# Two phases' projection work from a written list, and GpSimd multiplies and adds in a two-branch attention kernel

## The chip, the core and the metric

The kernel runs on one core of one Trainium2 chip. The metric is the device time of one execution in microseconds (us). TensorE is called PE below, VectorE DVE, ScalarE ACT, GpSimd POOL, and SyncE, whose queue issues nearly all DMAs, SP.

## What is computed

Two attention branches read two inputs of 2048 rows by 640 columns (bf16), each with 32 heads of 20 columns. Their outputs stand side by side.

```python
# branch A, for each of N = 4 segments of 512 rows
p     = softmax(q @ k.T * 20**-0.5 + causal mask within the segment)
a_dot = p @ v
pq    = phi(q)                              # t + 1 where t > 0, else exp(t)
a_mem = (pq @ M) / (pq @ z + 1e-6)
o     = g * a_mem + (1 - g) * a_dot         # g = sigmoid(beta), one per head
M, z  = M + phi(k).T @ v, z + phi(k).sum()  # M and z start at zero
# branch B
p = softmax of q @ k.T * 20**-0.5 over the last 256 rows up to the own one
o = p @ v
# each: o.reshape(2048, 640) @ wo
```

## The kernel before

**Phases, packs, slots.** Both branches are cut into 4 chunks of 512 rows. `body` (line 720) goes through eight phases in the order B0, A0, B1, A1, B2, A2, B3, A3. A phase's score work is cut into packs of up to 512 columns for four heads at once: 20 packs in B0 and in each A phase, 24 in B1 to B3. One turn of the loop over packs (line 739) is a slot, 172 in all; `self.slot` counts them. B0 has slots 0-19, A0 20-39, B1 40-63, A1 64-83, B2 84-107, A2 108-127, B3 128-151, A3 152-171.

**A slot.** It runs what was due in `self.after` (line 744), then the scores of its pack (`scores`, line 483), what stands in `self.behind`, one `weigh` if a unit (four heads of a chunk) has been complete for two slots, what stands in `last_of`, and then other work. `scores` issues 4 to 8 matmuls into two of three PSUM tiles `Sc`, two exponentials of 128x1024 on ACT (line 497) and the masks on POOL (lines 511, 517). `weigh` (line 527) multiplies the exponentials with v, copies the result from PSUM to SBUF on DVE (line 562; 577 in chunk 0), and SP transposes it by DMA. Four to six slots later `normalise` (line 591) divides: a reciprocal on DVE (595), a multiply (601) and, in A after chunk 0, an add of the memory's part `omem` (611). The multiply is on POOL in A1, A2 and A3 (`self.remembering`), on DVE elsewhere; the add is on DVE always, two to five groups of columns at once, at set groups.

**The other work.** It is a list per phase, `dense`, of pieces with a cost in us and sometimes a slot by which they are due, made by `plan` (line 385):

- `proj_padded` and `proj_rest` (lines 239, 263): B0's k and q.
- `proj` (line 287): one of five parts of k or q of a later chunk, five matmuls of 512 columns (A's are written Ak0 to Ak4 and Aq0 to Aq4 here, B1's Bk0 to Bq4). DVE copies it from PSUM (line 296), SP stores it to DRAM (297), and two slots after certain parts `spread` (line 306) loads groups of heads back in four DMAs, in the layout that the scores read. `cut` (line 298) says after which part which groups are loaded.
- `phi` (line 319): for A, one more exponential on ACT and two DVE operations per part, and for k a transposing DMA into `pkt`.
- `vproj` (line 349): one v tile of 128x320, DVE copies it.
- `load_x` (line 105): the next chunk's x, transposed by one DMA. Its tile has a single buffer per branch.

Two more kinds are kept apart: the memory's reads (`read`, line 447; eight in each of A1 to A3) and updates (`upd`, line 427; five per chunk of A but the last), and the output projection `out_half` (line 624). In each slot `body` takes as many pieces of the three kinds as `pick` (line 788) finds to fit best to a running sum of the costs; pieces that are due come first. So the order within a phase follows from costs and due slots.

**Queues and buffers.** Every engine and SP's queue run in program order. All these matmuls but the scores write to one kind of PSUM tile, `D`, with two buffers (line 235): the third writer waits for the copy of the first.

Of the kernel before, what the change touches and what calls it, by code (L numbers as in the profile page):

```python
# [8 lines left out]
ALU = mybir.AluOpType  # L9
# [8 lines left out]
G = 8  # L18
GW = 4 * DH
KT = 5  # L20
NC = 4
CH = 512
CT = CH // P
# [59 lines left out]
class Kern:  # L83
# [203 lines left out]
    def proj(self, br, c, which, m, st):  # L287
        nc = self.nc
        if m == 0:
            st[which] = self.dram.tile([KT * P, CH], BF16, name="%sd%s" % (which, br), bufs=2)  # L290
        ps = self.dtile([P, CH], F32)
        for kt in range(KT):
            nc.tensor.matmul(ps[:], lhsT=self.w[br + which][:, kt, m * P:(m + 1) * P],  # L293
                             rhs=self.xT[br][:, kt, :], start=(kt == 0), stop=(kt == KT - 1))
        t = self.wk.tile([P, CH], BF16, name="qk", bufs=4)
        nc.vector.tensor_copy(out=t[:], in_=ps[:])  # L296
        nc.sync.dma_start(out=st[which][m * P:(m + 1) * P, :], in_=t[:])
        cut = {1: (0, 3), 3: (3, 6), 4: (6, 8)} if (br, c) in (("A", 0), ("B", 1)) else {4: (0, 8)}
        if (br, c) == ("A", 1):
            cut = {2: (0, 4), 4: (4, 8)}  # L300
        if m in cut:
            self.at(self.slot + 2, lambda: self.spread(br, c, which, st, *cut[m]))
        if br == "A":
            self.phi(c, which, m, t, st)
# [80 lines left out]
    def plan(self):  # L385

        def kq(g, due):
            return [(1.25, lambda which=which: self.proj_padded(which, g), due) for which in "kq"]

        st = {}  # L390
        sr = {}

        def rest(what, due):
            return [(1.19, lambda: self.proj_rest(what, sr), due)]

        A = {(w, m): [self.a_kq("A", 0, w, m, st, {4: 9}.get(m))]
             for w in "kq" for m in range(KT)}
        stB = {}
        B = self.atoms_qk("B", 1, stB, True)
        upd = {c: [] for c in range(NC)}  # L400
        upd[0] = self.a_upd(0, st)
        v1 = self.a_v("B", 1, 0, 4)
        mix = [x for pair in zip(v1, upd[0]) for x in pair] + upd[0][4:]
        lists = [kq(0, 0) + kq(1, 2) + self.a_v("B", 0, 0, 4) + kq(2, 5) + rest("k0", 6)
                 + rest("q0", 6) + kq(3, 7) + rest("k1", 8) + rest("q1", 8) + rest("kq", 9)
                 + A["k", 0] + A["k", 1] + A["q", 0] + self.a_v("B", 0, 1, 14) + A["q", 1] + A["k", 2]
                 + A["q", 2] + A["k", 3] + A["q", 3],
                 self.a_v("A", 0, 0, 4) + self.a_x("B", 1) + A["k", 4] + A["q", 4]
                 + self.a_v("A", 0, 1, 14) + self.a_x("A", 1) + B,
                 [(x[0], x[1], 4) for x in mix]]  # L410
        for n in range(2, 7):
            br, c = "AB"[n % 2], (n + 1) // 2
            st = {}
            more = self.atoms_qk(br, c, st) + self.atoms_v(br, c)
            if br == "A":
                upd[c] = self.a_upd(c, st)
            if n == 2:
                more = (self.atoms_qk(br, c, st, True)[:6] + self.a_v("B", 1, 1, 13) + self.a_x("B", 2)
                        + self.atoms_qk(br, c, st, True)[6:] + self.atoms_v(br, c))
                lists[2] = lists[2] + more  # L420
            else:
                lists.append(more)
        return lists + [[]], upd
# [3 lines left out]
    def upd(self, c, m, st):  # L427
        nc = self.nc
        h0 = P * m // DH
        n = (P * (m + 1) - 1) // DH - h0 + 1  # L430
        W = DH + 1
        ps = self.dtile([P, 8, W], F32)
        for tt in range(CT):
            nc.tensor.matmul(ps[:, 0:n, :], lhsT=st["kt"][:, m, tt, :],
                             rhs=self.v["A"][0][:, tt, h0:h0 + n, 0:W],
                             start=(tt == 0), stop=(tt == CT - 1))
        if m == 0:
            self.mz[c] = self.wk.tile([P, KT, 8, W], BF16, name="mz", bufs=2)
        acc = self.macc[:, m, 0:n, :]
        bmb = self.bm[:, m, 0:n].unsqueeze(2).to_broadcast([P, n, W])  # L440
        if c == 0:
            nc.vector.tensor_copy(out=acc, in_=ps[:, 0:n, :])
        else:
            nc.vector.tensor_tensor(out=acc, in0=ps[:, 0:n, :], in1=acc, op=ALU.add)
        nc.vector.tensor_tensor(out=self.mz[c][:, m, 0:n, :], in0=acc, in1=bmb, op=ALU.mult)

    def read(self, c, tt, hf):
        nc = self.nc
        if tt == 0 and hf == 0:
            self.omem = self.io.tile([P, CT, D], BF16, name="omem", bufs=1)  # L450
        W = DH + 1
        ps = self.dtile([P, 16 * W], F32)
        cols = []
        for m in range(KT):
            h0 = P * m // DH
            h1 = (P * (m + 1) - 1) // DH
            prev = (P * m - 1) // DH if m else -1
            a, b = max(h0, 16 * hf), min(h1, 16 * hf + 15)
            if a > b:
                continue  # L460
            if a == prev and any(x[2] == prev for x in cols):
                cols.append((m, a, a, h0))
                a += 1
            if a <= b:
                cols.append((m, a, b, h0))
        for n, (m, a, b, h0) in enumerate(cols):
            nc.tensor.matmul(ps[:, (a - 16 * hf) * W:(b + 1 - 16 * hf) * W],
                             lhsT=self.phiq[:, m, tt * P:(tt + 1) * P],
                             rhs=self.mz[c - 1][:, m, a - h0:b + 1 - h0, :],
                             start=(n == 0), stop=(n == len(cols) - 1))  # L470
        pv = ps[:].rearrange("p (h e) -> p h e", e=W)
        hs = slice(16 * hf, 16 * hf + 16)
        rr = self.wk.tile([P, 16], F32, name="rm", bufs=2)
        nc.vector.scalar_tensor_tensor(out=rr[:], in0=pv[:, :, DH], scalar=EPS,  # L474
                                       in1=self.ge[:, hs], op0=ALU.add, op1=ALU.mult)
        nc.vector.reciprocal(out=rr[:], in_=rr[:])
        nc.vector.tensor_tensor(  # L477
            out=self.omem[:, tt, 320 * hf:320 * hf + 320].rearrange("p (h e) -> p h e", e=DH),
            in0=pv[:, :, 0:DH], in1=rr[:].unsqueeze(2).to_broadcast([P, 16, DH]), op=ALU.mult)
# [111 lines left out]
    def normalise(self, u, tp, a=0, n=CT):  # L591
        nc = self.nc
        pv = tp.rearrange("p b (j c) -> p b j c", j=4)
        rr = self.wk.tile([P, CT, 4], F32, name="rr", bufs=2)
        nc.vector.reciprocal(out=rr[:, 0:n, :], in_=pv[:, :, :, DH])
        if u.g == 0:
            self.o_tok[u.br, u.c] = self.io.tile([P, CT, D], BF16, name="ot" + u.br, bufs=2)
        o = self.o_tok[u.br, u.c][:, a:a + n, :]
        cols = slice(GW * u.g, GW * (u.g + 1))
        eng = nc.gpsimd if self.remembering else nc.vector  # L600
        eng.tensor_tensor(out=o[:, :, cols].rearrange("p b (j e) -> p b j e", j=4),
                          in0=pv[:, :, :, 0:DH],
                          in1=rr[:, 0:n, :].unsqueeze(3).to_broadcast([P, n, 4, DH]),
                          op=ALU.mult)
        if u.br == "A" and u.c > 0:
            c0 = {3: 0, 5: 4, 7: 6}.get(u.g, u.g + 1)
            if u.c == NC - 1:
                c0 = 0 if u.g == G - 4 else u.g if u.g > G - 4 else u.g + 1
            cols = slice(GW * c0, GW * (u.g + 1))
            if cols.stop > cols.start:  # L610
                nc.vector.tensor_tensor(out=o[:, :, cols], in0=o[:, :, cols],
                                        in1=self.omem[:, a:a + n, cols], op=ALU.add)
        if u.g == G - 1 and n == CT:
            self.tiles += [(u.br, u.c, tt) for tt in range(CT)]


# [103 lines left out]
    def body(self):  # L720
        phases = [Phase(br, c) for c in range(NC) for br in "BA"]
        lists, upd = self.plan()
        self.turned, self.half = [], []
        self.closing, self.open_masks = False, []
        for n, ph in enumerate(phases):
# [13 lines left out]
            for i, pk in enumerate(ph.packs):  # L739
# [20 lines left out]
                    f()  # L760
                if outs or i >= np_ - 3:
                    self.prefetch()
                part = sum(weights[:i + 1]) / sum(weights)
                can = 2 * sum(1 for t in self.turned if t[0] + 2 <= self.slot) + len(self.half)
                room, ahead, due = total * part - done, 0.0, 0.0
# [6 lines left out]
                for kind in self.pick(part, room, dense[at[0]:at[0] + 3],  # L772
# [5 lines left out]
                    else:  # L778
                        a = (dense, mem)[kind][at[kind]]
# [113 lines left out]
```

## Time and profile before

| what | value |
|---|---|
| three timed runs | 376.49, 377.37, 377.96 us; median 377.37 |
| profiled execution | 376.41 us, of which 374.7 are the span from the first to the last instruction |
| granted TensorE clock, mean | 0.995 |
| busy in slots 0-19 (10.33 to 54.27 us) | PE 41.85, ACT 36.35, DVE 28.20, POOL 29.84 of 43.94 |
| slots 20-39 (to 91.94) | PE 35.59, ACT 37.65, DVE 24.15, POOL 20.64 of 37.67 |
| slots 40-63 (to 142.92) | PE 45.95, ACT 49.22, DVE 42.22, POOL 41.05 of 50.98 |
| slots 64-83 (to 184.12) | PE 36.63, ACT 37.83, DVE 29.36, POOL 25.63 of 41.20 |
| slots 108-127 (233.22 to 274.11) | PE 36.37, ACT 37.77, DVE 29.07, POOL 25.59 of 40.89 |
| slots 152-170 (322.57 to 359.93) | PE 33.04, ACT 35.27, DVE 24.91, POOL 25.67 of 37.36 |

The stretches are cut where ACT's first exponential of a slot begins. Busy is the time in which an engine ran an instruction; a PE that is busy is not always at its peak, since matmuls overlap. A line of the timeline gives the start, the length, the engine, the line of the code, the operation with the tile it writes and the tiles it reads, how many were merged, and in brackets how long the engine had been idle before it and what ended that wait. A line of the waits gives who waited for whom, the total, how often, and the longest.

### The profile page before, as it was taken

The numbers are of one execution on the slowest core, as the hardware profiler recorded it, in microseconds if no ns is written. First come the engines' busy times: TensorE is split into PE (matmuls) and PEld (weight loads), VectorE is DVE, ScalarE is ACT, GpSimd is POOL, SyncE is SP. The second block draws the span as 40 slices with busy tenths as digits, with TensorE's granted clock in tenths as the row PEclk, the third lists the DMA queues.
The fourth block names the chain that finished last, engine by engine and source line by source line (L and its number), as shares of the span: only waits on it lengthen the run. The fifth ranks groups of instructions, "written<-read, shape, count | busy, mean of one in ns | idle before, by whom it ended". The sixth has DMA issues, their size and how long they took to land.

```text
span 374.7 us, 10400 instructions
## 1 busy us (share of the span) xinstructions
PE 337.9 (90%) x3930; PEld 159.5 (43%) x3930; DVE 261.7 (70%) x562; ACT 338.1 (90%) x386; POOL 262.2 (70%) x414
## 2 busy tenths in 40 slices
PE   8999999999898988898989999889899999989876
PEld 4443433433434344444434345334444444544444
DVE  2456767566888788866689877777567785776554
ACT  2778989999899998999899999999899999999943
POOL 9667675555786977566688889556678888766650
PEclk9999999999999999999999999999999999999989
DMA  8964457576434958566575976728644769465512
GB/s 250 311 231 118 115 162 167 120 197 155 129 98 136 175 129 161 158 111 128 83 174 131 198 125 112 155 58 154 114 86 119 140 156 114 97 133 118 131 41 73
DMA packets 112242, 52.08 MB, mean 139 GB/s; under 512 B 81856, under 2 KB 112192, under 8 KB 112192
## 3 DMA queue, kind: packets, MB, share of 16 engines
q1 hardware_dynamic: 112048, 51.33, 61.6%
q8 instruction: 31, 0.51, 0.6%
q14 instruction: 19, 0.16, 0.2%
q10 hardware_dynamic: 144, 0.08, 0.1%
HBM read 17.05 MB, written 15.07 MB: 86 GB/s over the span
## 4 chain that ended last, share of the span: by engine, by line
PE 45%; ACT 30%; DVE 11%; issue 6%; DMA 5%; POOL 2%; POOLq 0%; ACTq 0%; DVEq 0%
ACT pt L497 27%; PE D L293 14%; PE Sc L491 8%; PE D L353 5%; PE D L546 5%; PE D L630 4%; DMA ocT<-oc 3%; ACT pe L337 3%; DVE qk L296 2%; PE D L255 2%; DMA oT<-otB 2%; DVE oc L562 2%; PE Sc L674 1%; PE D L275 1%; DVE omem L477 1%
## 5 line engine op out<-in xcount | busy, mean ns | idle before, releaser
L497 ACT ACTIVATE pt<-Sc 128x1024 bf16<-128x1024 f32 (+1 forms) x344 | 321.4, 1072 | 19.9 <-PE Sc L491 18.7
L511 POOL TENSOR_SCALAR_AFFINE_SELECT pt<-pt 128x512 bf16<-128x512 bf16 x254 | 165.7, 664 | 94.3 <-ACT pt L497 93.9
L517 POOL TENSOR_SCALAR_AFFINE_SELECT pt<-pt 128x512 bf16<-128x512 bf16 x112 | 75.9, 691 | 3.4 <-ACT pt L497 3.1
L296 DVE CAST qk<-D 128x512 bf16<-128x512 f32 x70 | 48.2, 688 | 34.0 <-PE D L293 33.7
L491 PE MATMUL Sc<-qpB,kpB 20*128 20x256 bf16 (+2 forms) x704 | 47.8, 276 | 7.3 <-ACT pt L497 5.5
L562 DVE CAST oc<-D 128x512 bf16<-128x512 f32 x46 | 31.7, 690 | 16.5 <-PE D L546 16.1
L491 PE MATMUL Sc<-qpA,kpA 20*128 20x384 bf16 (+3 forms) x512 | 38.1, 301 | 2.7 <-ACT pt L497 2.3
L491 PEld LDWEIGHTS <-kpB 20*128 20x128 bf16 x704 | 15.1, 92 | 44.3 <-issue 42.9
L630 PEld LDWEIGHTS <-oT 128*128 128x128 bf16 x280 | 24.7, 98 | 20.0 <-issue 7.8
L633 DVE CAST ot<-D 128x320 bf16<-128x320 f32 x56 | 27.1, 486 | 7.5 <-PE D L630 6.5
L353 PE MATMUL D<-Bv,xTB 128*128 128x320 bf16 x160 | 25.5, 300 | 5.0 <-DVE oc L562 3.0
L630 PE MATMUL D<-Bo,oT 128*128 128x320 bf16 x160 | 26.5, 301 | 2.5 <-DMA oT<-otB 1.9
L546 PE MATMUL D<-pt,vB 128*32 128x384 bf16 (+2 forms) x720 | 26.3, 275 | 1.0 <-DVE qk L296 0.9
L293 PE MATMUL D<-xTA,Ak 128*128 128x512 bf16 x100 | 25.0, 381 | 1.8 <-DVE oc L562 1.8
L353 PE MATMUL D<-Av,xTA 128*128 128x320 bf16 x160 | 26.3, 301 | 0.3 <-DVE vA L361 0.2
L293 PE MATMUL D<-xTA,Aq 128*128 128x512 bf16 x100 | 25.0, 381 | 0.6 <-DVE phiq L577 0.3
L546 PE MATMUL D<-pt,vA 128*32 128x256 bf16 (+3 forms) x576 | 23.9, 291 | 1.5 <-DVE pkt L668 1.5
L491 PEld LDWEIGHTS <-kpA 20*128 20x128 bf16 x512 | 11.3, 92 | 30.6 <-issue 29.3
L630 PE MATMUL D<-Ao,oT 128*128 128x320 bf16 x120 | 20.2, 300 | 1.5 <-DVE rm L474 0.9
L337 ACT ACTIVATE pe<-qk 128x512 bf16<-128x512 bf16 x30 | 21.0, 704 | 0.0
L293 PE MATMUL D<-xTB,Bk 128*128 128x512 bf16 x75 | 18.7, 380 | 2.3 <-DVE omem L477 1.9
L353 PEld LDWEIGHTS <-xTB 128*128 128x128 bf16 x160 | 14.4, 97 | 14.0 <-issue 9.3
(103 smaller groups left out, 368.7 us busy)
## 6 DMA issues: line engine op xcount, KB each, us to landing
out_dram<-ot SPq DMA_DIRECT2D x31, 160.0 KB
kdA<-qk SPq DMA_DIRECT2D x20, 128.0 KB
qdA<-qk SPq DMA_DIRECT2D x20, 128.0 KB
kdB<-qk SPq DMA_DIRECT2D x17, 128.0 KB
qdB<-qk SPq DMA_DIRECT2D x17, 128.0 KB
kpB<-kdB SPq DMA_DIRECT2D x8, 160.0 KB
qpB<-qdB SPq DMA_DIRECT2D x8, 160.0 KB
kpA<-kdA SPq DMA_DIRECT2D x8, 160.0 KB
```

The source lines that it names most:

```text
L293: nc.tensor.matmul(ps[:], lhsT=self.w[br + which][:, kt, m * P:(m + 1) * P], rhs=self.xT[br][:, kt, :], start=(kt == 0), stop=(kt == KT - 1))
L296: nc.vector.tensor_copy(out=t[:], in_=ps[:])
L337: nc.scalar.activation(out=e[:], in_=t[:], func=ACT.Exp)
L353: nc.tensor.matmul(ps[:, 0:320], lhsT=self.xT[br][:, kt, tt * P:(tt + 1) * P], rhs=self.w[br + "v"][:, kt, hf * 320:(hf + 1) * 320], start ...
L491: nc.tensor.matmul(ps[j // 2][:, j % 2, off * P:(off + nq) * P], lhsT=kp[rows, u.g, k0:k0 + P], rhs=self.qp[u.br][rows, u.g, q0 * P:(q0 + ...
L497: nc.scalar.activation(out=pt[:, 2 * hp:2 * hp + 2, 0:pk.used], in_=ps[hp][:, :, 0:pk.used], func=ACT.Exp, scale=SCALE)
L511: nc.gpsimd.affine_select(out=blk, in_=blk, pattern=[[0, 4], [1, P]], compare_op=ALU.is_ge, fill=0.0, base=0, channel_multiplier=-1)
L517: nc.gpsimd.affine_select(out=blk, in_=blk, pattern=[[0, 4], [-1, P]], compare_op=ALU.is_ge, fill=0.0, base=-1, channel_multiplier=1)
L546: nc.tensor.matmul(O[32 * j:32 * j + 32, q0 * P:(q0 + nq) * P], lhsT=v[:, kt % CT, v0:v0 + 32], rhs=pt[:, j, off * P:(off + nq) * P], star ...
L562: nc.vector.tensor_copy(out=oc[:], in_=O[:])
L630: nc.tensor.matmul(ps[:, 0:320], lhsT=st["oT"][:, m, :], rhs=self.w[br + "o"][:, m, hf * 320:(hf + 1) * 320], start=(m == 0), stop=(m == K ...
L633: nc.vector.tensor_copy(out=st["ot"][:, hf * 320:(hf + 1) * 320], in_=ps[:, 0:320])
```

## The change

It does three things.

**A written list for the first two phases.** For B0 and A0 `pick` and the due slots are no longer used: `self.fixed` names the pieces of each of the 40 slots, and `body` runs them in place of the choice. By it the slots hold:

- Slots 0-19: the same pieces as before but Aq3. Ak0 comes in slot 9 (before 10), the last `proj_rest` in 10 (8), Aq0 in 13 (11), Ak1 in 14 (11), Aq1 in 15 (15), Ak2 in 17 (17), Aq2 in 18 (17), Ak3 in 19 (18). No slot after slot 5 has more than one projection.
- Slots 20-39: Aq3 in 22 (before 18), Aq4 in 23 (24), Ak4 in 25 (23), the load of B1's x in 25 (23), Bk0 in 27 (28), Bq0 in 28 (30), A1's x in 31 (28), the other projections of B1 but Bk4 and Bq4 up to slot 38, and all five updates of chunk 0 in slots 34, 36, 36, 39, 39 (before 41 to 44).
- Slots 40-63: `pick` again. Bk4 and Bq4 come in 43 and 44 (before 38 and 39); the rest moves by up to five slots until slot 54. From slot 55 on the projections, reads, updates and outputs stand in the slots where they stood.

**Spread of A's first q.** Its groups are now loaded 0-2, 3, 4-7 (after parts 1, 2, 4), before 0-2, 3-5, 6-7 (after 1, 3, 4).

**POOL in A.** In A1 to A3 the updates' multiply goes to POOL. The add of `omem` is made per group, one slot after the multiply, on the engine of the multiply, and not before all eight reads are done; in A3 that puts the adds of groups 0 to 2 into slot 166. A3's groups 5 to 7 have both on DVE.

The diff without what only renames:

```diff
+        if (br, c, which) == ("A", 0, "q"):
+            cut = {1: (0, 3), 2: (3, 4), 4: (4, 8)}
...
+        self.fixed = [
+            [[k[1], q[1], vB[0][0]], vB[0][1:3], [vB[0][3], k[2]], [q[2]], [r["k0"]],
+             [r["q0"], k[3]], [q[3]], [r["k1"]], [r["q1"]], [Ak[0]],
+             [r["kq"]], [vB[1][0]], vB[1][1:3], [vB[1][3], Aq[0]], [Ak[1]],
+             [Aq[1]], [], [Ak[2]], [Aq[2]], [Ak[3]]],
+            [vA[0][0:2], [vA[0][2]], [vA[0][3], Aq[3]], [Aq[4]], [vA[1][0]],
+             xB + [Ak[4]], [vA[1][1]], [Bkq[0]], [Bkq[1]], [vA[1][2]],
+             [Bkq[2]], [vA[1][3]] + xA, [Bkq[3]], [Bkq[4]], u0[0:1],
+             [Bkq[5]], u0[1:3], [Bkq[6]], [Bkq[7]], u0[3:5]]]
+        lists = [[(x[0], x[1], 0) for x in kq(0, 0)], [],
+                 self.a_v("B", 1, 0, 4) + [(x[0], x[1], 9) for x in Bkq[8:]]]
...
-        nc.vector.tensor_tensor(out=self.mz[c][:, m, 0:n, :], in0=acc, in1=bmb, op=ALU.mult)
+        eng = nc.gpsimd if self.remembering else nc.vector
+        eng.tensor_tensor(out=self.mz[c][:, m, 0:n, :], in0=acc, in1=bmb, op=ALU.mult)
...
-        eng = nc.gpsimd if self.remembering else nc.vector
+        pool = self.remembering and (u.br == "B" or u.c < NC - 1 or u.g < 5)
+        eng = nc.gpsimd if pool else nc.vector
...
+        def add():
+            if self.reads < 2 * CT:
+                self.at(self.slot + 1, add)
+                return
+            eng.tensor_tensor(out=o[:, :, cols], in0=o[:, :, cols],
+                              in1=self.omem[:, a:a + n, cols], op=ALU.add)
+
         if u.br == "A" and u.c > 0:
-            c0 = {3: 0, 5: 4, 7: 6}.get(u.g, u.g + 1)
-            if u.c == NC - 1:
-                c0 = 0 if u.g == G - 4 else u.g if u.g > G - 4 else u.g + 1
-            cols = slice(GW * c0, GW * (u.g + 1))
-            if cols.stop > cols.start:
-                nc.vector.tensor_tensor(out=o[:, :, cols], in0=o[:, :, cols],
-                                        in1=self.omem[:, a:a + n, cols], op=ALU.add)
+            if pool:
+                self.at(self.slot + 1, add)
+            else:
+                add()
...
+                if n < len(self.fixed):
+                    for a in self.fixed[n][i]:
+                        a[1]()
+                    self.slot += 1
+                    continue
```

`a_x` is the piece that calls `load_x`, `a_upd` the five updates, `self.reads` counts the memory's reads of a phase.

More of the change, by code (lines that the diff above doesn't have):

```diff
@@ L394, in rest @@
             return [(1.19, lambda: self.proj_rest(what, sr), due)]
-        A = {(w, m): [self.a_kq("A", 0, w, m, st, {4: 9}.get(m))]
-             for w in "kq" for m in range(KT)}
+        Ak, Aq = [[self.a_kq("A", 0, w, m, st) for m in range(KT)] for w in "kq"]
         stB = {}
-        B = self.atoms_qk("B", 1, stB, True)
+        Bkq = self.atoms_qk("B", 1, stB, True)
         upd = {c: [] for c in range(NC)}
[L401 to L410, printed above, removed]
+        u0 = self.a_upd(0, st)
+        vB, vA = [[self.a_v(br, 0, hf) for hf in range(2)] for br in "BA"]
+        xB, xA = self.a_x("B", 1), self.a_x("A", 1)
+        k, q = [[kq(g, None)[i] for g in range(4)] for i in range(2)]
+        r = {w: rest(w, None)[0] for w in ("k0", "q0", "k1", "q1", "kq")}
+        self.fixed = [
[9 more added lines that the diff above has]
+                 self.a_v("B", 1, 0, 4) + [(x[0], x[1], 9) for x in Bkq[8:]]]
         for n in range(2, 7):
@@ L417, in plan @@
             if n == 2:
-                more = (self.atoms_qk(br, c, st, True)[:6] + self.a_v("B", 1, 1, 13) + self.a_x("B", 2)
+                more = (self.atoms_qk(br, c, st, True)[:6] + self.a_v("B", 1, 1, 15) + self.a_x("B", 2)
                         + self.atoms_qk(br, c, st, True)[6:] + self.atoms_v(br, c))
@@ L449, in read @@
         if tt == 0 and hf == 0:
+            self.reads = 0
             self.omem = self.io.tile([P, CT, D], BF16, name="omem", bufs=1)
+        self.reads += 1
         W = DH + 1
@@ L604, in normalise @@
                           op=ALU.mult)
-        if u.br == "A" and u.c > 0:
-            c0 = {3: 0, 5: 4, 7: 6}.get(u.g, u.g + 1)
-            if u.c == NC - 1:
-                c0 = 0 if u.g == G - 4 else u.g if u.g > G - 4 else u.g + 1
-            cols = slice(GW * c0, GW * (u.g + 1))
-            if cols.stop > cols.start:
-                nc.vector.tensor_tensor(out=o[:, :, cols], in0=o[:, :, cols],
-                                        in1=self.omem[:, a:a + n, cols], op=ALU.add)
+        def add():
[4 more added lines that the diff above has]
+                              in1=self.omem[:, a:a + n, cols], op=ALU.add)
+        if u.br == "A" and u.c > 0:
+            if pool:
+                self.at(self.slot + 1, add)
+            else:
+                add()
         if u.g == G - 1 and n == CT:
+            assert not pool or u.br == "B"
             self.tiles += [(u.br, u.c, tt) for tt in range(CT)]
```

## The prediction

> **What bounds the kernel.** I read the page first, then the waits, then the timeline of ScalarE (ACT) slot by slot, and at each hole in it the timeline of all engines. A slot is one turn of the loop over packs (172 in all: 0-19 B0, 20-39 A0, 40-63 B1, 64-83 A1, 84-107 B2, 108-127 A2, 128-151 B3, 152-171 A3).
>
> ```profile
> PE 337.9 (90%) x3930; PEld 159.5 (43%) x3930; DVE 261.7 (70%) x562; ACT 338.1 (90%) x386; POOL 262.2 (70%) x414
> ```
>
> ACT and PE are both at 90%. Two exponentials back to back take 1.81 us (slots 77.07, 78.89, 80.70 in the chain that ended last), 0.52 more where an exponential of phi joins them, and almost everywhere they follow one another. So a change can win only what ACT idles.
>
> ```profile
> ACT pt L497 <- PE Sc L491: 18.7, 25, 1.6
> ...
> DVE otA L611 <- POOL otA L601: 6.5, 4, 2.2
> ```
>
> Put to slots, the holes between ACT's first and last score exponential are 7.6 us in slots 0-19, 0 in 20-39, 1.8 in 40-63, 3.4 in 64-83, 0.1 in 84-107, 3.1 in 108-127, 1.4 in 128-151, 2.1 in 152-171. The largest holes outside slots 0-19 have one shape; slot 81:
>
> ```profile
> 176.29 0.73 POOL L601 TENSOR_TENSOR otA<-ocT,rr 128x320 bf16<-128x320 bf16 x1
> ...
> 177.05 0.82 DVE L611 TENSOR_TENSOR otA<-otA,omem 128x1280 bf16<-128x1280 bf16 x1 [1.43 <-POOL otA L601]
> ...
> 177.80 0.68 DVE L562 CAST oc<-D 128x512 bf16<-128x512 f32 x1
> ...
> 178.53 1.52 PE L353 MATMUL D<-Bv,xTB 128*128 128x320 bf16 x10 [1.50 <-DVE oc L562]
> ...
> 180.50 3.77 ACT L497 ACTIVATE pt<-Sc 128x1024 bf16<-128x1024 f32 x4 [1.26 <-PE Sc L491]
> ```
>
> The DVE add waits 1.43 for GpSimd's multiply, a PSUM copy stands behind it, PE waits 1.50 for that buffer (there are two), ACT 1.26 for PE. Slot 41 is the same with other work ahead of the copy:
>
> ```profile
> 94.01 0.97 DVE L601 TENSOR_TENSOR otA<-omem,rr 128x320 bf16<-128x320 bf16 x1
> ...
> 94.91 0.68 DVE L577 CAST phiq<-D 128x512 bf16<-128x512 f32 x1
> ...
> 95.63 0.84 PE L353 MATMUL D<-Bv,xTB 128*128 128x320 bf16 x5 [0.99 <-DVE phiq L577]
> ...
> 96.92 3.77 ACT L497 ACTIVATE pt<-Sc 128x1024 bf16<-128x1024 f32 x4 [1.21 <-PE Sc L491]
> ```
>
> SyncE's queue (SP) is the third thing: from 26 to 75 us it issues with hardly a gap, 0.33 per piece and 1.2 to 2.8 per transposing load, and the instruction order lets eight DMAs be in flight.
>
> **The parts, in order of the run.** Sums are against the profiled execution: 376.41 us, a span of 374.7 and 1.7 around it. The three timed runs have their median 0.96 higher (377.37), which I add at the end.
>
> Slots 0-19. PE loses one projection (1.25) and the pairs in slots 4, 7, 11, 17, 18 are spread out. The holes there are 1.21, 0.66, 1.60, 0.62, 0.39, so 4.5 by PE alone. But the scores of slot 12 need the spread of q groups 5-6, and those of slot 20 the spread of A's groups 0-2. In the trace both stood on SP: slot 20's four matmuls take 1.62 instead of 0.4 because the last q piece, issued at 51.68, landed at 53.90 by the trace's completion marks.
>
> ```profile
> 52.69 1.62 PE L491 MATMUL Sc<-qpA,kpA 20*128 20x512 bf16 x4
> ...
> 69.81 1.24 PE L293 MATMUL D<-xTB,Bk 128*128 128x512 bf16 x5
> ```
>
> Up to that piece the new SP order has 57 issues where the old has 58, and the Aq1 store now stands ahead of A's first spread. Walking SP with its own durations puts q 5-6 at 37.7 (37.9 before) and the piece for slot 20 at 53 to 54.5. So nearly all of the gain waits for SP: -0.5, bounds -1.5 and +0.5.
>
> Slots 20-28, a new wait. B's next x load moves from slot 23 to 25 and its first reader, Bk0, from slot 28 to 27. On SP it now stands behind the spread of q groups 4-7, which waits for the store of Aq4 (slot 23). Before, it had this place:
>
> ```profile
> 60.55 1.26 SPq L580 DMA_TRANSPOSE phiq<-phiq  x1
> 61.91 2.53 SPq L107 DMA_TRANSPOSE xTB<-in_B_x_dram  x1
> 64.53 0.54 SPq L297 DMA_DIRECT2D kdA<-qk  x1
> ```
>
> It landed at 66.55, 3.3 before its reader at 69.81. Now, from Aq4's start on PE: matmuls 1.25, copy 0.7 and gaps 0.2, store to landing 1.9 to 2.2, four spread issues 1.45 to 1.6, x load 4.64 to 5.81 (the five later x loads of the trace), 0 to 0.5 for SP being busy: 10.1 to 12.1, I take 10.6, nearest to the 4.64 load of this very stretch. In the trace slot 23's projection begins at 59.45 and slot 27's dense work at 67.29; ACT would be fed if Bk0 (1.2) and the scores behind it (0.4) ended with slot 27's exponentials, that is if Bk0 began 8.1 to 8.9 after Aq4. So ACT idles 1.2 to 4.0; I take +2.2. Queued behind Bk0 on PE are all later scores, so nothing hides it.
>
> Slots 28-39. One projection fewer than before with five memory updates more (0.44 of PE each): PE stays under 1.9 a slot. The updates cost DVE 0.30+0.38 each. Slot 36 has most: 0.24+0.49, copy 0.69, two updates 1.36, so 2.8; slot 37 then 1.4, slot 38 0.7: 4.9 in three slots of 1.81. Covered, and 0.3 to 0.6 per double slot if not. Spreading the rest wins a little (slots 28, 31, 34, 39 exceed 1.81 by 0.15 to 0.27): -0.2, bounds -0.4 and +1.2.
>
> Slots 40-63. The five updates leave slots 41-44, where DVE needs 10.1 us in 10.9 (slots 39-44); without them 7.3 in 9.1 (39-43). Two projections (2.4 of PE) come in place of 2.2 of updates, and the balance by slot is as good. The 1.8 of holes go but for a rest: -1.5, bounds -0.5 and -1.8.
>
> Slots 64-83 and 108-127. The DVE add of four columns is gone with its wait; five adds of 128x320 and five multiplies of 128x147 are new on GpSimd. The trace has neither there. Add: from 0.33 (the DVE add of that size) to 1.45 (two of GpSimd's 0.73 multiplies); I take 0.73, the same engine and shape. Multiply: 0.38 (DVE, same shape) to 0.73; I take 0.4, what 0.73 scaled by width gives (0.33) and a little more. GpSimd in its fullest stretch (slots 73-77): eight masks 4.9, two multiplies 1.46, two adds 1.46, four updates 1.6: 9.4 in 9.1 us, so its masks come 0.3 late, and PE reads them a slot later. DVE's next copy in slot 80 then follows the matmuls directly (176.7 instead of 178.5), PE goes on at 176.97 and ACT's 1.26 closes, in both phases: -2.5, bounds 0 and -2.6. The other holes there (memory reads filling both PSUM buffers) stay.
>
> [...]
>
> Slots 84-107 and 128-151. The doubled DVE adds (0.73, 0.80) of groups 4-5 and 6-7 become single ones of 0.33. They stand ahead of the copies PE waits for in slots 130 (0.58, hole 0.63) and 135 (0.42, hole 0.44): -0.8, bounds 0 and -1.1.
>
> Slots 152-171. Memory reads end in slot 165, so three adds fall together in slot 166 (2.2 on GpSimd), the fourth in 167, the fifth in 170. The masks of slot 166 come 1.2 late, but PE waits 1.52 for an oT transpose in slot 169 anyway. The DVE add of 1.40 with 2.25 of wait goes; group 5 stays on DVE (0.49+0.33 instead of GpSimd's 0.73 and a wait of 1.34), so the copies before the last weighing come about 0.8 earlier, while the fifth add ends at about 358.9, 0.3 later than PE asked for those columns: -0.5, bounds -1.0 and +1.0.
>
> Sum: -0.5 +2.2 -0.2 -1.5 -2.5 -0.8 -0.5 = -3.8, so 372.6 in a profiled execution and **373.6** as a median.
>
> **Rivals.** (1) x arrives in time: SP has slack I do not see and Bk0 does not wait. For it: before, the load had 3.3 to spare. Against it: the chain above is by dependences, 10.1 at the least. Time 373.6 - 2.2 = 371.4. (2) The A phases give nothing back, because the next limit is already there: B2's and B3's q pieces landed at 181.88, and with the hole closed slot 84's scores ask at about 182.3, so 0.4 is all the room; or PE, busy 36.6 of 41.2 us in slots 64-83, fills the hole. Then 373.6 + 2.5 = 376.1. (3) Slower: GpSimd falls behind. Its queue is in order, so late adds make masks late, and PE's weighing waits two slots later with all scores behind it. It decides when an add costs over about 1.1: at 1.45, with updates at 0.8, slots 73-77 hold 12.5 in 9.1; less the 1.0 that the two-slot lag forgives, 2.4 lost in each A phase, and 2.5 in slots 166-171 where four adds stand together. 373.6 + 2 x 2.4 + 3.0 (2.5 and the 0.5 not won) = 381.4. For it: GpSimd is busy 1.33 of 1.82 there already. Against: the nearest row is 0.73. (4) The list doesn't do what it says: the order of instructions shows that it does.
>
> [...]
>
> **How the numbers follow.** Forecast 0.5, with its own range 371.9 to 375.3; rival 1 0.15; rival 2 0.2; rival 3 0.13; 0.02 left. A measurement of this kernel can tell about 0.5% (1.9 us) from no change, so faster means under 375.5. Faster: 0.5 + 0.15 and a little of rival 2, less the forecast's upper edge: 0.65. Same: most of rival 2 and that edge, 0.2. Slower 0.15. The range takes in rivals 1 and 2 and the bounds around them, 370.2 to 378.2, and leaves out most of rival 3.
>
> **What would show it.** Right: PE waiting 2 to 4 us for the DMA of xTB before Bk0 in slot 27 and a hole of about 2 in ACT there, the only one in slots 20-39; slot 20 beginning within 1 us of 54.3; no DVE wait for GpSimd's otA; no hole at slots 41-43, 81, 125. Wrong: GpSimd adds over 1.1 each, PE waiting for masks in L546, slot 84 waiting for qpB, or Bk0 without a wait.

## The result, and the profile after

The changed kernel takes **380.69 us** (median of six runs, 379.99 to 384.50), the kernel before beside it 376.62: a ratio of 1.011, 95% interval 1.0072 to 1.0148. Six further runs on another chip gave 1.0172 (1.0115 to 1.023). It is slower by about 1 to 2%. The forecast was 373.6 and the range ended at 378.2: both were wrong. (Medians here are over all executions of a kernel; the ratios leave out those more than 1.5% above its fastest.) The profiled execution is the longest of the six, 384.50 us with a span of 382.5; a second profile, of a run of 383.34 us, stands beside it in the table.

The first part of the page and the row of the granted clock, after:

```profile
PE 341.0 (89%) x3891; PEld 159.5 (42%) x3930; DVE 259.2 (68%) x552; ACT 339.0 (89%) x386; POOL 275.3 (72%) x438
...
PEclk9999998899999989999999999889999999999999
```

and the row of before:

```profile
PEclk9999999999999999999999999999999999999989
```

POOL is busy 13 us more than before and DVE 2.5 less. The new thing is the clock. Before, it was below full once, near the end. After, the row has 8s in five places. In the records under this row each is a stretch of 3.41 us in which the clock granted to PE was 0.5: from 57.26, 74.33, 139.18, 238.17 and 248.41 us on.

Against before, by slots (differences in us; the second column of results is the second profile):

| slots | forecast | after | again |
|---|---|---|---|
| 0-19 | -0.5 | +1.24 | +1.17 |
| 20-27 | +2.2 | +6.09 | +4.23 |
| 28-39 | -0.2 | -0.07 | +1.05 |
| 40-57 | -1.5 (40-63) | -2.04 | -1.92 |
| 58-63 | | +2.78 | +3.27 |
| 64-83 and 108-127 | -2.5 | -1.28 | -2.95 |
| 84-107 and 128-151 | -0.8 | +2.92 | +2.07 |
| 152 to the end | -0.5 | -1.96 | -0.86 |

The time went to four places, and at each the same thing is seen. The view of the waits (who waited for whom, total, times, longest) names them:

```profile
ACT pt L507 <- PE Sc L501: 26.3, 33, 3.1
...
DVE rr L605 <- DMA ocT<-oc: 7.1, 5, 2.1
...
PE D L293 <- DMA xTB<-in_B_x_dram: 3.1, 1, 3.1
...
PE Sc L501 <- DMA qpA<-qdA: 2.0, 3, 0.9
```

ACT waits for PE 26.3 us where it was 18.7. Three rows down are DMAs that land late. The timeline of PE and of SP's queue at slot 20 (start, length, engine and line, in brackets the idle time before it and what ended it):

```profile
52.19 2.28 SPq L319 DMA_DIRECT2D qpA<-qdA  x4
...
54.37 0.37 PE L501 MATMUL Sc<-qpA,kpA 20*128 20x512 bf16 x1 [0.92 <-DMA qpA<-qdA]
55.13 0.37 PE L501 MATMUL Sc<-qpA,kpA 20*128 20x512 bf16 x1 [0.39 <-DMA qpA<-qdA]
56.16 0.51 PE L501 MATMUL Sc<-qpA,kpA 20*128 20x512 bf16 x2 [0.65 <-DMA qpA<-qdA]
56.60 2.25 PE L355 MATMUL D<-Av,xTA 128*128 128x320 bf16 x10
```

Each of the four scores of slot 20 waits for its own q piece. The line after them is the one to look at: ten matmuls take 2.25, where ten such take 1.52 in the lines of before (178.53). From 57.26 on PE runs at half clock. The same at slot 27:

```profile
69.14 2.72 SPq L107 DMA_TRANSPOSE xTB<-in_B_x_dram  x1
...
74.08 2.10 PE L293 MATMUL D<-xTB,Bk 128*128 128x512 bf16 x5 [3.10 <-DMA xTB<-in_B_x_dram]
...
76.84 3.95 ACT L507 ACTIVATE pt<-Sc 128x1024 bf16<-128x1024 f32 x4 [3.05 <-PE Sc L501]
```

This is the wait that was forecast, 3.10 long; but Bk0 then takes 2.10 and not 1.24. Third, the timeline of SP ahead of slot 58, where nothing was forecast:

```profile
127.37 1.39 SPq L297 DMA_DIRECT2D qdA<-qk  x1
131.09 1.43 SPq L319 DMA_DIRECT2D qpA<-qdA  x4
132.62 1.20 SPq L574 DMA_TRANSPOSE ocT<-oc  x1
133.91 2.77 SPq L107 DMA_TRANSPOSE xTB<-in_B_x_dram  x1
```

and what DVE and PE then do:

```profile
136.35 0.25 DVE L605 RECIPROCAL rr<-ocT 128x16 f32<-128x16 bf16 x1 [2.11 <-DMA ocT<-oc]
...
138.93 1.28 PE L355 MATMUL D<-Av,xTA 128*128 128x320 bf16 x5 [2.02 <-DVE qk L296]
```

SP stands from 128.8 to 131.09 until Aq2's store has landed, the ocT transpose behind it starts at 132.62, DVE waits 2.11 for it, and PE 2.02 for DVE's copy. The fourth place, slot 105, has the same chain:

```profile
235.17 0.25 DVE L605 RECIPROCAL rr<-ocT 128x16 f32<-128x16 bf16 x1 [2.06 <-DMA ocT<-oc]
...
236.71 0.84 PE L355 MATMUL D<-Av,xTA 128*128 128x320 bf16 x5 [2.01 <-DVE vA L363]
```

What was moved to GpSimd did nearly as forecast. Its groups (count, then busy time and mean ns of one):

```profile
L621 POOL TENSOR_TENSOR otA<-otA,omem 128x320 bf16<-128x320 bf16 x15 | 12.0, 804 | 0.0
...
L453 POOL TENSOR_TENSOR mz<-macc,bmask 128x147 bf16<-128x147 f32 x8 | 3.5, 434 | 0.0
```

An add takes 0.80 (0.73 was taken), an update's multiply 0.43 (0.4). The holes at slots 81 and 125 are gone; the line that stands for before's hole of 1.26 is now one run of 16 exponentials:

```profile
172.70 15.06 ACT L507 ACTIVATE pt<-Sc 128x1024 bf16<-128x1024 f32 x16
```

### The profile page after: what moved, and what is told of

It is laid out like the page before. It is cut to its first block, busy times and chain, and to the rows that moved or that the text cites. A ratio compares the mean times of both kernels' runs of the same rounds, so it can differ in the third digit from the quotient of the medians.

```text
span 382.5 us, 10341 instructions
## 1 busy us (share of the span) xinstructions
PE 341.0 (89%) x3891; PEld 159.5 (42%) x3930; DVE 259.2 (68%) x552; ACT 339.0 (89%) x386; POOL 275.3 (72%) x438
## 4 chain that ended last, share of the span: by engine, by line
PE 45%; ACT 23%; DVE 15%; DMA 6%; issue 6%; POOL 4%; SPq 1%; ACTq 0%; POOLq 0%; DVEq 0%
ACT pt L507 21%; PE D L293 15%; PE Sc L501 8%; PE D L556 6%; PE D L355 6%; DMA ocT<-oc 4%; DVE qk L296 3%; PE D L647 3%; PE D L255 2%; POOL pt L521 2%; DVE oc L572 2%; PE D L275 2%; ACT pe L339 1%; DMA xTB<-in_B_x_dram 1%; DVE otA L612 1%
## 5 line engine op out<-in xcount | busy, mean ns | idle before, releaser
L507 ACT ACTIVATE pt<-Sc 128x1024 bf16<-128x1024 f32 (+1 forms) x344 | 322.7, 1072 | 29.1 <-PE Sc L501 26.3
L501 PE MATMUL Sc<-qpA,kpA 20*128 20x384 bf16 (+3 forms) x512 | 37.9, 306 | 2.9 <-DMA qpA<-qdA 2.0
L355 PE MATMUL D<-Av,xTA 128*128 128x320 bf16 x160 | 28.8, 317 | 4.6 <-DVE qk L296 2.5
L556 PE MATMUL D<-pt,vB 128*32 128x384 bf16 (+2 forms) x720 | 27.2, 285 | 1.2 <-DVE qk L296 1.1
L293 PE MATMUL D<-xTA,Ak 128*128 128x512 bf16 x88 | 24.2, 381 | 3.3 <-DVE oc L572 2.2
L293 PE MATMUL D<-xTB,Bk 128*128 128x512 bf16 x65 | 20.1, 414 | 5.9 <-DMA xTB<-in_B_x_dram 3.1
L361 DVE CAST vB<-D 128x320 bf16<-128x320 f32 x32 | 15.6, 489 | 9.2 <-PE D L355 8.8
```

The lines of the kernel that those rows point to most:

```text
L355: nc.tensor.matmul(ps[:, 0:320], lhsT=self.xT[br][:, kt, tt * P:(tt + 1) * P], rhs=self.w[br + "v"][:, kt, hf * 320:(hf + 1) * 320], start ...
L501: nc.tensor.matmul(ps[j // 2][:, j % 2, off * P:(off + nq) * P], lhsT=kp[rows, u.g, k0:k0 + P], rhs=self.qp[u.br][rows, u.g, q0 * P:(q0 + ...
L507: nc.scalar.activation(out=pt[:, 2 * hp:2 * hp + 2, 0:pk.used], in_=ps[hp][:, :, 0:pk.used], func=ACT.Exp, scale=SCALE)
L556: nc.tensor.matmul(O[32 * j:32 * j + 32, q0 * P:(q0 + nq) * P], lhsT=v[:, kt % CT, v0:v0 + 32], rhs=pt[:, j, off * P:(off + nq) * P], star ...
```

## The theories

**Theory 1**: the loss is made by a few DMAs that land late (slots 12, 20, 27, 58), and by the half clock that these waits of PE bring on (0.92 + 0.39 + 0.65, 3.10, 2.02 and 2.01 above). **Theory 2**: the waits alone cost the time; the drops of the clock come by chance. **Theory 3**: the work moved to GpSimd makes the loss.

## Experiments: which part of the change

**The list alone** (in the changed kernel, A's multiplies and adds as before):

```diff
-        eng = nc.gpsimd if self.remembering else nc.vector
-        eng.tensor_tensor(out=self.mz[c][:, m, 0:n, :], ...)
+        nc.vector.tensor_tensor(out=self.mz[c][:, m, 0:n, :], ...)
-        pool = self.remembering and (u.br == "B" or u.c < NC - 1 or u.g < 5)
+        eng = nc.gpsimd if self.remembering else nc.vector
```

> The written list and the cut of A's first q alone; multiply and adds in A as before. Theory 1 (the loss comes from PE standing still for DMAs in slots 20 and 27, and from the half clock that follows each such hole): the changed kernel's loss without what GpSimd wins, so 380.7 + 2.5 (the holes at 81 and 125 come back) = 382 to 384, and ACT's slot 40 at 98 to 100 us. Theory 3 (GpSimd's new work in A makes the loss): under 379.

387.21 us, ratio 1.017 (1.01 to 1.0241), more than the 382 to 384 expected. It loses what the changed kernel loses, and slots 64-83 and 112-127 are back at 41.57 and 32.14 (before 41.20 and 32.13). Slot 40 began at 96.4, not at 98 to 100: slot 20 was on time in this profile.

**GpSimd's part alone** (the kernel before, with the lines taken out above):

> The GpSimd part alone (multiply of the updates, adds one by one, A3's last groups on VectorE); both first phases as before. Theories 1 and 2 (the loss is in the first phases): 376.6 - 2.5 = 373.5 to 375, no hole at slots 81 and 125, granted clock above 0.99. Theory 3: 378 or more, with holes in slots 105 to 112.

376.78 us against 378.61 beside it, ratio 0.9918 (0.9877 to 0.996); slot 81 has no hole, slots 112-127 take 30.77 (before 32.13). Theory 3 falls: this part is a gain of 0.8%, and the list loses about twice that. (Times of the kernel before differ by chip, so ratios are compared from here on.)

**The changed kernel again**, on one chip with the next two:

> The changed kernel itself once more, beside the next three on one chip. Theory 1 (DMA waits of PE in slots 20, 27 and 58, each with a chance of a half-clock stretch behind it): about 4 us over the kernel before, mean granted clock 0.977 to 0.987 against 0.99; its runs with few half-clock stretches are the short ones.

383.78, ratio 1.0172 (1.0115 to 1.023): more than the 4 us expected. The mean granted clock of its runs is 0.973 to 0.982 (0.991 to 0.995 in most runs of the kernel before); its profile is the last column of the table above.

## Experiments: the wait or the clock

**x early**:

```diff
-             [vA[0][0:2], ..., [Aq[4]], [vA[1][0]], xB + [Ak[4]], ...
+             [vA[0][0:2], ..., xB + [Aq[4]], [vA[1][0]], [Ak[4]], ...
```

> The changed kernel with the load of B1's x in slot 23, ahead of Aq4's store, in place of slot 25. Bk0 then finds x landed. Theory 1 (wait and the half clock behind it): the 3.05 hole goes and the 0.85 by which Bk0 is longer, and about 1 us more of work at half clock behind it: 380.7 - 4.5 = 375.5 to 377. Theory 2 (the waits alone, the clock's drops come by chance): 380.7 - 2.5 = 377.7 to 378.5. Slot 20's late q stays in both.

380.01, ratio 1.0015 (0.9977 to 1.0054); on the scale of the expectations (the kernel before at 376.62) 377.2, between the two. Bk0 does not wait for x any more:

```profile
64.66 2.58 SPq L107 DMA_TRANSPOSE xTB<-in_B_x_dram  x1
...
70.27 1.24 PE L293 MATMUL D<-xTB,Bk 128*128 128x512 bf16 x5 [0.22 <-DVE omem L587]
```

Slots 24-27 take 7.74 and not 11.00. So the load's place cost 3.26 in the profiled run.

**PE kept busy, no DMA earlier**:

```diff
+    def fill(self, ps, n):
+        w = self.w["Bk"]
+        for _ in range(n):
+            self.nc.tensor.matmul(ps, lhsT=w[:, 0, 0:P], rhs=w[:, 0, 0:CH], start=True, stop=True)
...
+        if (br, c, which, m) == ("B", 1, "k", 0):
+            self.fill(ps[:], 12)
...
+        if self.slot == 20:
+            self.fill(ps[0][:, 0, :], 8)
```

> The changed kernel, with matmuls of no use put where PE stood still: 8 of 128x512 ahead of the scores of slot 20 and 12 ahead of Bk0, all on weights that are long loaded, into tiles that are overwritten. The DMAs come no earlier. Theory 1: PE has no hole over 2 us in slots 19 to 27, so no half clock at 57 and 74 us; slots 20 to 24 lose about 2.5 less and slots 27 to 29 about 1.0 less: 380.7 - 3.5 = 376.5 to 378. Theory 2: the waits are the same and the time too, 380 to 382, with half-clock stretches at the same places or none that matter.

379.5, ratio 1.0044 (1.0009 to 1.0078), or 378.3 on the same scale: just over theory 1's 378. The first half-clock stretch of its profile is at 241.67; there is none in slots 0 to 63, and its mean granted clock is 0.995 (0.976 and 0.978 in the two profiles of the changed kernel). Slots 20-27 take 18.23, against 21.22 and 19.36 in the two profiles of the changed kernel and 16.00 with x early: PE still waits for the same DMAs, and time was won with work that nobody needs. That speaks for theory 1, though the changed kernel ran on other chips. So the same test was made cleanly, on the best kernel (told below), all on one chip ("the first kernel" of the two expectations that follow): x loaded late, alone and filled.

```diff
-                 self.a_v("A", 0, 0, 4) + self.a_x("B", 1) + A["k", 4] + A["q", 4]
+                 self.a_v("A", 0, 0, 4) + A["k", 4] + A["q", 4]
+        self.at_end(26, lambda: self.load_x("B", 1))
```

> The first kernel of this call with one thing changed: B1's x is loaded at the end of slot 26's scores, behind the spread, in place of slot 23, and Bk0 (slot 28) has to wait about 3 us for it, as in the change. Theory 1 (the wait, and PE at half clock behind it): slots 24 to 31 longer by 4 to 5.5, the time too. Theory 2 (the wait alone): 2 to 3 longer, full clock or no effect of it.

> As the last one, with 12 matmuls of no use (128x512, on weights long loaded, into the tile that Bk0 overwrites) ahead of Bk0. x lands no earlier. Theory 1: PE is not idle, so no half clock in slots 27 to 30, and the time is 2 to 3 over the first kernel of this call, 1.5 to 2.5 under the one without the filling. Theory 2: as the one without the filling, or longer.

Timed: without the late load 372.99 (ratio 0.9836, 0.9775 to 0.9898), late 379.60 (0.9997, 0.9957 to 1.0036), late and filled 376.86 (0.9956, 0.9918 to 0.9994). So by the medians the wait costs 3.9, and 2.7 more go when PE is kept busy; both are more than theory 1 expected of the time. The mean granted clock of the executions says the same: 0.9965 without the late load, 0.9867 late, 0.9945 late and filled. The timelines, late:

```profile
76.72 0.61 PE L293 MATMUL D<-xTB,Bk 128*128 128x512 bf16 x1 [3.95 <-DMA xTB<-in_B_x_dram]
77.55 1.49 PE L293 MATMUL D<-xTB,Bk 128*128 128x512 bf16 x3 [0.22 <-issue]
...
79.67 2.85 ACT L501 ACTIVATE pt<-Sc 128x1024 bf16<-128x1024 f32 x3 [5.38 <-PE Sc L495]
```

and filled:

```profile
72.39 2.75 PE L492 MATMUL D<-Bk 128*128 128x512 bf16 x11
77.09 1.24 PE L295 MATMUL D<-xTB,Bk 128*128 128x512 bf16 x5 [1.95 <-DMA xTB<-in_B_x_dram]
...
78.75 3.77 ACT L508 ACTIVATE pt<-Sc 128x1024 bf16<-128x1024 f32 x4 [4.68 <-PE Sc L502]
```

x lands even later in the filled one (Bk0 5.11 after slot 28's start, not 4.56), yet ACT goes on 1.66 after Bk0's start and not 2.95. The busy times of slots 28-31, with the granted clock behind them, of the kernel without the late load, late, and filled:

```profile
71.70:79.39 7.69, 7.33 (x83) 3.07 (x83) 4.10 (x8) 7.69 (x9) 3.73 (x6) 1.00 0.86 143
```

```profile
72.16:85.26 13.10, 8.88 (x83) 3.21 (x84) 4.26 (x8) 7.72 (x9) 3.74 (x6) 0.74 0.80 145
```

```profile
71.98:84.35 12.37, 10.12 (x95) 4.19 (x95) 4.27 (x8) 7.69 (x10) 3.74 (x6) 1.00 0.78 153
```

The same 83 matmuls are 8.88 of work at a mean clock of 0.74 and 7.33 at 1.00. Theory 2 falls: the drop follows the hole and goes when the hole is filled. How much time it costs is less sure. In these two profiles slots 28-31 differ by 0.73, or 1.29 with x landing at the same point, where the medians differ by 2.7.

## Experiments: which DMA, and why late

**x and q early**: as x early, and Aq1 changed over with Ak1, so that the first q spread no longer stands behind Ak1's transposing load.

```diff
-             ... [vB[1][3], Aq[0]], [Ak[1]],
-             [Aq[1]], ...
+             ... [vB[1][3], Aq[0]], [Aq[1]],
+             [Ak[1]], ...
```

> The changed kernel with B1's x in slot 23 ahead of Aq4 and with Aq1 and Ak1 changed over (Aq1 in slot 14, Ak1 in 15), so that A's first q is loaded before Ak1's transposing load stands in SP's queue. Theory 1: no hole in slot 27, slots 20 to 23 take 7.4 and not 10.2, slot 28 begins at most 1 us after that of the kernel before; slot 58 still waits. 0 to 1 us over the kernel before, so -3 to -4 against the changed kernel. Theory 2 (the order of SP matters only through chance): no different from the kernel with x alone early.

379.74, ratio 0.9983 (0.993 to 1.0035), hardly less than with x alone. In the next kernel, which has the same order, slots 20-23 take 8.89 and not 7.4, and slot 20 waits for the last k piece in place of q (0.60): two spreads of four issues each and a transposing load have to pass SP in those slots, and changing two of them over only changes which is last. So this expectation failed.

**B2's x early as well** (the change had moved the due slot of B1's second half of v from 13 to 15, in a line that the diff above does not print):

```diff
-                more = (... + self.a_v("B", 1, 1, 15) + self.a_x("B", 2)
+                more = (... + self.a_v("B", 1, 1, 13) + self.a_x("B", 2)
```

> As the last one, and B1's second half of v due by slot 13 of its phase again (15 in the change): by that Aq2 of the next chunk comes in slot 50 and its q is loaded from slot 52, B2's x in 53. Theory 1 (slot 58's wait comes from SP standing for the store of Aq2, 131.09 instead of 120.45): slots 58 to 63 take 11.9 and not 14.65, and the time is 1 to 2 below the last one, 1 to 2 below the kernel before. If slot 58's wait were chance: as the last one.

378.15, ratio 0.9995 (0.9955 to 1.0034): the 1 to 2 us expected below the last kernel do not show in the time. But slots 58-63 take 11.90, where the changed kernel has 14.65 and 15.14 and the kernel before 11.87. Its SP order there:

```profile
126.67 1.20 SPq L574 DMA_TRANSPOSE ocT<-oc  x1
127.97 2.94 SPq L107 DMA_TRANSPOSE xTB<-in_B_x_dram  x1
```

The ocT is issued 5.87 before slot 58's start (132.54) and not 3.77 before it (136.38), and the reciprocal that reads it waits for nothing. So the wait of slot 58 comes from one due slot in the change (15 for 13), by which the fit put Aq2 a slot later, and from how long the store of Aq2 then takes to land, since the spread behind it waits for that. By the completion marks it took 2.02 in one profile with due 15, where slots 58-63 take 12.04, and 2.80 to 3.70 in four others, where they take 13.44 to 15.14. In eight profiles with due 13 it took 1.93 to 2.08, and these slots 11.88 to 11.90.

What is left of the loss is in slots 12 to 23: slot 12 now waits for q groups 5-6 (1.53, 0.19 and 0.33) and a half-clock stretch follows at 39.15 (the ten matmuls from 38.74 on take 2.49, where such ten take 1.53 in the profile after). That of slot 12 is not the list's alone: the fastest kernel, which has no list, waits there too (0.18 and 0.22) and has a stretch at 39.23 (seven such matmuls from 39.40 on take 2.05, 1.11 in the trace of before).

## Experiments: without the list

**The updates in A0, placed by the fit**:

```diff
+        tail = B[0:4] + [x for pair in zip(u0, B[4:8]) for x in pair] + u0[4:]
...
-                 + self.a_v("A", 0, 1, 14) + self.a_x("A", 1) + B,
-                 [(x[0], x[1], 4) for x in mix]]
+                 + self.a_v("A", 0, 1, 14) + self.a_x("A", 1) + tail,
+                 v1 + [(x[0], x[1], 9) for x in B[8:]]]
```

> No written list: the kernel before, with the GpSimd part, with the five updates of chunk 0 among the last pieces of A0 and Bk4 and Bq4 in B1, each placed by the cost fit. Theory 1: the 2 us of slots 40 to 57 and the 2 to 3 of the A phases are won and no DMA wait is new: 376.6 - 4.5 = 371.5 to 373, the fastest so far. If the list itself gave the 2 us of slots 40 to 57: 374, as with GpSimd's part alone.

375.24 against 378.92, ratio 0.9921 (0.9884 to 0.9957): in time no more than GpSimd's part alone (0.9918), so theory 1's 371.5 to 373 did not come. In its profile slots 40-57 do take 37.81 (before 39.11), 1.3 of the list's 2.0, but the timed runs do not show a gain from the updates' place. The largest hole left near the end, 1.66 of ACT in slot 170, is GpSimd's:

```profile
357.13 0.73 PE L674 MATMUL D<-ident,otA 128*128 128x128 bf16 x10 [1.88 <-POOL otA L614]
```

**A3's groups 3 and 4 on VectorE too**:

```diff
-        pool = self.remembering and (u.br == "B" or u.c < NC - 1 or u.g < 5)
+        pool = self.remembering and (u.br == "B" or u.c < NC - 1 or u.g < 3)
```

> The last kernel (no written list; GpSimd part; updates in A0) with groups 3 and 4 of A3 on VectorE too, so that GpSimd's last adds no longer stand before the last transposes. If those adds make the 1.66 hole of slot 170 and the 0.7 of slot 168: 375.2 - 1.5 = 373 to 374.5. If the holes there have another cause (masks, the last transposes themselves): 375 to 376.

372.99, ratio **0.9836** (0.9775 to 0.9898), the fastest kernel of the study. Slots 152-170 take 37.08 and not 38.14. The rest of what it has over the previous kernel is across chips and not settled.

**The list for B0 put back into that one** (and the cut of A's first q; A0 by the fit):

> The same as the one before (A3 on VectorE), with the change's written list for B0 alone and its cut of A's first q; A0 by the cost fit, x early. Theory 1 (the loss of the list's first phase is in q pieces that land late for slots 12 and 20, with half clock behind): slots 0 to 23 take 53 to 54.5 and not 51.2, so 2 to 3.5 slower than the kernel without the list. Theory 2 (B0's list is good for the 0.5 forecast, and all its loss came from slots 27 and 58): 0 to 0.5 faster than the kernel without.

377.71, ratio 0.9928 (0.9884 to 0.9972): 0.9% behind the kernel without it by the ratios, whose intervals still overlap a little (its times run from 372.27 to 383.56), and 376.0 against 374.0 by the profiled spans. In the profiles slots 20-23 are 1.18 longer, PE waiting 0.88 and 0.34 for qpA; slots 0-19 only 0.32, because slot 12 was late in the kernel without the list as well. So theory 2 of that expectation is unlikely but not ruled out, and the numbers given for theory 1 (51.2 without, 53 to 54.5 with) did not come either: 53.80 and 55.30.

## Why the prediction was wrong, step by step

The terms add up to -3.8; the two profiles give +7.8 and +6.7. Two things failed. The path of the DMAs through SP was walked for slots 12, 20 and 27 only, and taken too short for slot 20; a later store, and all that stands behind it, was given nothing in slots 40-63 and 84-107. And the half clock behind the holes of PE, five times 3.41 us at 0.5 in the first profile, has no term at all.

- **Slots 0-19**, "Walking SP with its own durations puts q 5-6 at 37.7 (37.9 before) and the piece for slot 20 at 53 to 54.5. So nearly all of the gain waits for SP: -0.5": failed in the landing. The last piece for slot 20 landed at 56.25 and 56.22 by the completion marks, 1.7 beyond the later end: the k spread, issued from 43.82 on before, was now issued from 47.99 on, with two transposes behind it and ahead of q. In the six profiles with this order it landed at 54.98 to 57.33, in the six that keep the old order of B0 at 53.12 to 55.67. The loss shows in slots 20-23: 8.19 to 10.21 in all profiles with the list, 7.23 to 7.39 without it (9.38 once, with a half-clock stretch). Slots 0-19 themselves, +1.24 and +1.17, decide nothing: they take 43.70 to 46.87 with the list and 43.93 to 47.00 without.
- **Slots 20-28**, "So ACT idles 1.2 to 4.0; I take +2.2": the wait came where forecast, with a hole of 3.05, so rival 1 fell. The chain from Aq4 to Bk0 took 10.25 (63.83 to 74.08), where 10.6 was taken (its upper end adds up to 12.3, not 12.1). What is missing is the 0.8 to 2.8 lost in slots 20-23, and the clock. With PE kept busy, slots 24-27 take 9.84 against 7.74 with x early: the wait is 2.10, the term almost to the point. The 1.0 to 1.3 above that in the kernels without filling (10.87 to 11.17) had no term.
- **Slots 28-39**: -0.07 in the first profile, right. No run shows the waits that the upper bound of +1.2 allows for: the five moved update multiplies took 0.32 or 0.33 each, none longer beside a mask. In the second profile (+1.05) a half-clock stretch, from 72.05 on, reaches into them.
- **Slots 40-63**, "the balance by slot is as good": this counted PE and DVE and did not follow SP. Slots 40-57 won 2.04, more than the 1.5; slots 58-63 lost 2.78 by an Aq2 one slot later, whose store landed late.
- **Slots 64-83 and 108-127**: right in mechanism and size: -2.15 with GpSimd's part alone, -2.95 in the second profile; in the first a half-clock stretch in slots 108-111 took 1.25 back. Rivals 2 and 3 fell: the two phases did become shorter, and an add at 0.80 is under rival 3's 1.1. (Rival 3's 381.4 puts back the 0.5 of the last term but not the 2.5 of this one.)
- **Slots 84-107 and 128-151**, "The doubled DVE adds [...] become single ones of 0.33": failed. The holes of slots 130 and 135 stayed, 0.59 and 0.70 (0.63 and 0.44 before). The timeline of slot 135:

```profile
296.18 0.96 DVE L612 TENSOR_TENSOR otA<-ocT,rr 128x320 bf16<-128x320 bf16 x1
...
296.75 0.88 POOL L521 TENSOR_SCALAR_AFFINE_SELECT pt<-pt 128x512 bf16<-128x512 bf16 x1
...
297.17 0.64 DVE L621 TENSOR_TENSOR otA<-otA,omem 128x320 bf16<-128x320 bf16 x1
...
298.46 0.84 PE L556 MATMUL D<-pt,vB 128*32 128x384 bf16 x24 [0.68 <-DVE qk L296]
```

  The single add takes 0.64, as all six of its kind do (0.63 or 0.64, a mask running on GpSimd during each), and the normalise 0.96: together 1.60, where before the normalise took 0.79 and the double add 0.80. The forecast's 0.33 is the time of an add with nothing running on GpSimd (360.45 in the trace of before; 0.32 at 373.73 in that of after). By these rows the 0.31 more of the add and the 0.17 more of the normalise ate the whole term. Of the +2.94 in slots 84-107, 2.80 are the late ocT of slot 105. The chain is that of slot 58: the q spread ahead of this ocT waits for the store of the last q. That store took 3.2 to 3.9 to land in seven profiles whose slots 104-107 take over 9, and 1.7 to 2.7 in six where they take under 8. The list does not decide it alone: the two fastest kernels, which differ in A3 alone, take 7.25 and 10.15 there. But of six profiles with the list for both phases five are over 9, of six without any list one, so it may make the late landing likelier. Why the store takes longer stays open.
- **Slots 152 to the end**, -0.5: -1.96 and -0.86. In slots 152-170 the adds on GpSimd cost 0.86 in place of a gain (without groups 3 and 4 there, 1.06 less), the price that was bounded at +1.0. Behind slot 170 the second profile is 1.71 shorter than before, though both have a half-clock stretch there (369.01; before 360.82). Among what is gone there is DVE's wait of 1.34 for GpSimd's group 5; no run takes this gain apart. The first profile, which has no stretch there until its last microsecond, is 1.11 shorter still.
- **The slower case** was given 0.15 on one mechanism, GpSimd, that did not come; the one that came was in none of the rivals, though its sign stood in the page of before, the one 8 in the row of the clock.

## What to carry to other kernels

Before a transfer is moved or delayed, walk its queue for everything behind it, and count, for a wait of PE like those here (3.10, 2.02 and 2.01 in the changed kernel, 3.95 with x late), with the half clock that was seen behind each of them. A list that is made by PE's durations alone moves stores and the loads behind them as well. Of a change in several parts, run each alone: here a gain of 0.8% was hidden by a loss twice as large, and the one place where the list gained in the profiles, that of the updates, needed no list.

## What the runs showed of the hardware

**The granted clock.** In the traces of before and after every half-clock stretch, but for the one that each execution ends in, lasts 3.41 us. After's begin 17.07, 64.85, 98.99 and 10.24 apart, which are 5, 19, 29 and 3 times 3.413, and the last one 133.12 (39 times) behind them; before's two are 13.65 apart (4 times). Cut at that spacing from PE's first matmul on, the two traces have these stretches at full clock in which PE ran matmuls for less than 2.1 of the 3.41 (without the one ahead of each execution's last half clock), and one more that a half clock followed:

```
trace    from     PE busy   half clock next
before   357.40   1.52      yes
before   353.99   1.89      no
before   176.50   1.91      no
before   265.24   1.92      no
after     53.85   1.84      yes
after     70.91   0.32      yes
after    135.77   1.40      yes
after    234.75   1.46      yes
after    367.87   1.91      no
after    244.99   2.21      yes
```

So in these two traces a half clock stands behind each of the five with 1.84 or less, and behind none of the four with 1.89 to 1.92. The wait of PE alone does not tell it: that of 1.91 before 369.38 falls on two stretches, and no half clock follows. Nor is PE's time the whole condition: a half clock follows the 2.21 at 244.99, among the memory's reads of slot 110, and none the 2.19, 2.20 and 2.26 from 145.78, 186.74 and 156.02 on in before, nor the 2.25 from 193.79 on in after; this is not explained. The scatter of executions goes with the clock. In the 69 executions of the kernel before that the experiments' ratios rest on, the 38 with a mean granted clock of 0.993 or more took 377.4 on average, the 23 around 0.991 379.1, the 8 at 0.986 or less 379.5. A stretch of 3.41 at half clock lowers the mean by 0.0045 (half of 3.41 in 377); the slope is 0.9 us for each stretch there, and 1.9 and 1.2 in the two sets of six executions of the changed kernel, holes and clock together. Those 12 have a mean of 0.9798, the 69 of 0.9931: by estimate 3.0 stretches more, 2.7 to 5.5 us by these slopes, which is the size of the loss (4.1 beside each other).

**GpSimd and VectorE.** An add of 128x320 (bf16) takes 0.80 on GpSimd (mean of 15). On VectorE it took 0.33 in the tail of the kernel before, and 0.63 or 0.64 in all six places in slots 84-107 and 128-151 after the change, beside GpSimd's masks: the forecast had taken 0.33 for these.
